# Scan, attention and a three-way gated layer on one core: the last part's product turned round, its result copied in halves, and a new order of the first two parts

## The chip, the core and the metric

One Trainium2 chip, one of its cores. Five engines work side by side, each with its own queue of instructions taken in order: TensorE (PE, with its weight loads, PEld), VectorE (DVE), ScalarE (ACT), GpSimd (POOL) and SyncE (SP), which here issues most transfers. They wait for one another by semaphores. The metric is the device time of one execution in microseconds (us).

## The reference

```python
def _attn_ref(r, k, v, w, u):              # r, k, v, w: (4, 8, 768, 48), u: (8, 48)
    state = zeros((B, H, D, D))
    for t in range(S):
        kt, vt, rt, wt = (k[:, :, t], v[:, :, t], r[:, :, t], w[:, :, t])
        cur = einsum('bhd,bhe->bhde', u[None] * kt, vt)
        y[:, :, t] = einsum('bhd,bhde->bhe', rt, state + cur)
        state = wt[:, :, :, None] * state + einsum('bhd,bhe->bhde', kt, vt)

def _moe_ref(x, w1, w2, w3, w_out):        # x: (3072, 384), w1..w3: (384, 768), w_out: (768, 384)
    h = maximum(maximum(x @ w1, x @ w2), x @ w3)
    return h @ w_out
```

The result of the recurrence, laid out as 3072 tokens by 384, is the input of the layer.

## The kernel before

**Tiling.** The recurrence is cut into 24 chunks (k = 0 to 23): six stretches of 128 time steps for each of four batches. The layer is cut into six parts ("halves" in the code) of 512 tokens; part h needs the four chunks of its stretch of time. For each part there are 18 products up (three weight matrices by six tiles f of 128 hidden columns), of which the maximum of three is tile f of h, and then the products down. Most layer products are done as three products of a high and a low half each (hi x hi, hi x lo, lo x hi); in part 0 the tiles f below 4 are done as one full product.

**The order.** The first two parts and the chunks up to 13 are issued by a written list, PARTS (line 79), read left to right; every engine takes its share of each step into its own queue in that order. After it a loop (line 802) issues parts 2 to 5 and the other chunks. The letters of the list, with the chunk's number behind them:

- Chunks: `n` loads (SP, L267). `b`, `f` scans (DVE, L406, L421), with `p` (POOL, L415) and `q` (DVE, L418) between. `r` scales r and k (DVE, L430). `c3` squares for a later check (ACT, L435). `d` multiplies k by u, for k below 8 in four ACT instructions (L443). `e` for k below 8 is 32 small products (PE, L460) and a copy (DVE, L463), then the loads of the next chunk's v (SP). `X` scores (PE, L489), `M` their copy (DVE, L496, and for some chunks ACT, L500, other columns of the same tile `grams`). `T` transposes (PE, L511; ACT copies to kn, L513). `R`, `V`, `Y` write the chunk's y (PE, L527, L593, L614); behind `V` ACT reads four elements (the touch, L598, L620), for which `Y` waits. `U` products for the state (PE, L551, L542), `m`, `S`, `Z` the state itself (L558, L563 or L566, L570). `E` copies y into x (ACT, L632, L636).
- Weights: `w` issues a load (SP, L329). `l` converts a pair of loaded weights (two ACT instructions, L346 and L347). `h` is DVE's part of it (L352), ahead of which it issues the conversions of a pair if `l` has not. `c` alone joins them (DVE, L358). `s` and `o` split a pair in high and low (ACT, DVE, L140, L141).
- Layer: `g` with a piece and a number is a group of products up of part 0 (`d`: the columns of chunks 0 and 1, `c`: of chunks 2 and 3, `e`: all), `G` of part 1, `D` and `H` are groups down of parts 0 and 1 (L211). `t` takes one finished group out of PSUM (ACT copy L158 the first time, DVE maximum L160 after). `x` splits x. `W10` is ten filler products on PE (L660).

Ahead of the list stand LEAD fillers of one column and WARM full ones (line 789). `grams` is a PSUM tile of two banks.

**The end.** In the last part the product down has h as the standing operand and w_out as the moving one (384 columns), so that rows are tokens: four tiles tt of 128 tokens. Tiles 0 and 1 are copied by ACT and stored by SP (L216, L765); tiles 2 and 3 (`late`) stay in PSUM. Behind the last group come BACK one-column fillers. Then every engine reads a flag (L820) and jumps over a second, slow way of computing everything (L821), which is there for inputs that the fast way cannot do. Behind the jump ACT copies tile 2 and DVE copies tile 3 (L932), and SP stores both (L933).

Of the kernel before, what the change touches and what calls it, by code (L numbers as in the profile page):

```python
# [44 lines left out]
C = 128  # L45
# [22 lines left out]
WARM = 9  # L68
LEAD = 69
BACK = 8  # L70
# [8 lines left out]
PARTS = """b0 w w p0 q0 f0 d0 b1 e0 p1 q1 R0 w d1 r0 W10 X0 c0 w T0 f1 W3 M0 b2 n3 p2 e1 r1 V0 q2 U0 W3 d2 l w X1 f2 w Y0 E0 M1  # L79
         T1 n4 h e2 R1 V1 r2 c1 c Y1 U1 w b3 E1 R2 X2 S1 l p3 T2 w M2 gd0 q3 d3 U2 V2 n5 h f3 c e3 c2 Y2 S0 t gd1 r3  # L80
         gd3 l T3 t X3 b4 p4 gd2 d4 E2 n6 U3 h q4 S2 M3 t c f4 R3 S3 e4 r4 V3 h gd4 gd5 c3 c T4 Y3 E3 Z4 X4 d5 t c4 U4
         M4 m4 b5 gd6 t w t gd7 p5 w q5 R4 n7 V4 S4 t b6 e5 f5 t gc1 t r5 gc7 Z5 p6 gc0 d6 t Z6 gc4 w t l T5 Y4 h X5
         c5 c w U5 q6 gc3 M5 f6 l gc2 b7 ge9 m5 E4 t p7 S5 gc5 h t c R5 q7 t h c e6 d7 r6 t x h V5 ge11 s gc8 t T6 l
         X6 o Y5 c h U6 ge10 ge13 t s o w t ge14 h w M6 m6 c E5 t s c o f7 S6 t t c6 Z7 n8 ge15 R6 V6 e7 h t gd8 w b8
         c ge16 ge12 r7 p8 ge17 w t t h c7 T7 X7 c l Y6 U7 E6 t d8 gc6 t t q8 s o l n9 D3 f8 D0 m7 s b9 Z8 r8 D4 p9 S7
         T8 R7 M7 q9 w f9 o V7 X8 Z9 Y7 U8 E7 n10 m8 e8 D1 l c8 D5 s x b10 d9 p10 l S8 o M8 D2 G12 r9 s t G13 G2 G0 t
         G14 G1 e9 o s t c9 T9 R8 V8 n11 w t X9 b11 q10 Y8 E8 f10 l U9 G4 t G3 o d10 w p11 m9 q11 t r10 e10 S9 M9 w
         f11 Z10 G6 c10 s l t G16 t r11 w T10 R9 o V9 n12 b12 t w p12 t w X10 s U10 M10 t Y9 o G15 q12 t G5 f12 t s
         Z11 o r12 G17 E9 d11 m10 S10 t t t s t G10 G7 T11 T12 e11 R10 V10 t d12 X11 Z12 U11 Y10 n13 G8 G9 c12 o c11
         m11 S11 M11 G11 t E10 R11 e12 t V11 X12 t U12 b13 t Y11 t E11 p13 H2 H5 H3 m12 x q13 H0 H1 w d13 H4 f13 M12  # L90
         n14 r13 e13 Z13 S12 c13"""
# [8 lines left out]
LATE = 2  # L100
# [12 lines left out]
def kernel(ctx: ExitStack, tc, tin, nat, u_flat, u_pair, v_t, w_flat, out, ytr):  # L113
# [16 lines left out]
    across = out[0:NH - 1].rearrange("h (k p t) -> h k p t", k=KT, p=128)  # L130
    natural = out[NH - 1].rearrange("(b p n) -> b p n", b=B, n=DM)
# [12 lines left out]
    def moe(x, pools, store, late=None, plain=0, turned=True):  # L144
# [7 lines left out]
        def take_up(f, ps, cols):  # L152
# [3 lines left out]
            n = taken[f, cols.start] = taken.get((f, cols.start), 0) + 1  # L156
# [42 lines left out]
        def downs():  # L199
            order = [(tt, f) for tt in range(KT if turned else CPH) for f in range(FT)]  # L200
            order.insert(FT, order.pop(FT - 1))
            wide_to = HT if turned else DM
            pss = {}
            for n, (tt, f) in enumerate(order):
# [4 lines left out]
                for i, (ht, wt) in enumerate(terms):  # L209
                    h, w = ht[f], wt[FT * 3 + f]  # L210
                    nc.tensor.matmul(pss[tt][:, 0:wide_to], lhsT=w[:, cut] if turned else h[:, cut],  # L211
                                     rhs=h[:, :] if turned else w[:, :],
                                     start=(f == 0 and i == 0), stop=(f == FT - 1 and i == len(terms) - 1))
                if f == FT - 1 and not (late and tt >= LATE):
                    o = mp.tile([128, HT], F32, name="m")[:, 0:wide_to]
                    nc.scalar.copy(out=o, in_=pss[tt][:, 0:wide_to])  # L216
                    store(tt, o)
# [603 lines left out]
    with tc.If(rv != 0), ExitStack() as slow:  # L821
# [99 lines left out]
        with tc.For_i(0, NH - 1) as half:  # L921
            again_moe(half, across, True)
# [80 lines left out]
```

## Time and profile before

| | us |
|---|---|
| median of three runs | 391.71 |
| the three runs | 391.2, 391.71, 394.22 |
| the profiled execution | 391.18 |
| its span, first to last instruction | 389.5 |
| PE busy in it | 381.7 (98%) |
| DVE busy | 265.9 (68%) |
| ACT busy | 173.4 (45%) |
| POOL busy | 85.2 (22%) |

An instruction's row names the line, the engine, the operation, and out<-in by the program's names. Idle time in square brackets or behind the bar is that of the engine ahead of the instruction, with what ended it. A "q" behind an engine's name is its sequencer.

### The profile page before, as it was taken

How to read it: one execution, taken by the hardware profiler on the slowest of the kernel's cores; microseconds unless marked ns; L12 is line 12 of the kernel's file. 1: busy time of each engine (PE TensorE's matmuls, PEld its weight loads, DVE VectorE, ACT ScalarE, POOL GpSimd, SP SyncE). 2: the span in 40 equal slices, each digit the busy share in tenths (PEclk: the TensorE clock that was granted, in tenths of full speed). 3: DMA queues.
4: the chain of work that ended last, by engine and by line, in shares of the span. 5: the costliest groups of instructions: out<-in, count | busy, mean ns of one | idle time of the engine just before them, and what ended most of it. 6: DMA issues, size and time to landing. Idle time of an engine off the chain costs nothing.

```text
span 389.5 us, 10503 instructions
## 1 busy us (share of the span) xinstructions
PE 381.7 (98%) x4480; PEld 309.3 (79%) x4480; DVE 265.9 (68%) x399; ACT 173.4 (45%) x373; POOL 85.2 (22%) x102
## 2 busy tenths in 40 slices
PE   8899999999999999999999999999999999999995
PEld 4688867766788888888888888888888887878895
DVE  7999999986779975598778567777568431432320
ACT  4688787643544443333444443443443332421210
POOL 3000000221443252144424314333414100000000
PEclk9999999999999999999999999999999999999999
DMA  7993897301823431477243866143951123200002
GB/s 284 403 347 103 284 406 248 112 2 52 272 68 126 147 127 51 136 292 223 68 173 115 275 198 210 61 168 98 307 201 44 42 82 89 94 3 1 0 24 67
DMA packets 23576, 58.44 MB, mean 150 GB/s; under 512 B 2720, under 2 KB 3712, under 8 KB 23520
## 3 DMA queue, kind: packets, MB, share of 16 engines
q1 hardware_dynamic: 20144, 48.58, 36.0%
q10 hardware_dynamic: 3376, 9.09, 7.3%
q8 instruction: 37, 0.61, 0.6%
q14 instruction: 19, 0.16, 0.1%
HBM read 51.87 MB, written 4.72 MB: 145 GB/s over the span
## 4 chain that ended last, share of the span: by engine, by line
PE 86%; DVE 6%; DMA 3%; ACT 2%; issue 2%; SPq 0%; POOL 0%; ACTq 0%; DVEq 0%
PE psm L175 53%; PE psm L211 18%; PE grams L489 3%; PE y L527 3%; PE y L614 3%; DMA w<-in_w_all_dram 2%; PE psm L511 2%; PE grams L542 1%; DVE w L358 1%; PE grams L460 1%; DVE cv L352 1%; PE grams L211 1%; PE y L211 1%; DMA tin<-in_tin_dram 1%; DVE w L141 1%
## 5 line engine op out<-in xcount | busy, mean ns | idle before, releaser
L175 PE MATMUL psm<-x_hi,w 128*128 128x512 f32 x576 | 183.0, 393 | 0.0
L175 PEld LDWEIGHTS psm<-x_hi,w 128*128 128x128 f32 x576 | 108.1, 188 | 23.5 <-issue 0.2
L175 PE MATMUL psm<-x_lo,w 128*128 128x512 f32 x288 | 112.1, 389 | 0.0
L160 DVE TENSOR_TENSOR m<-psm,m 128x512 f32<-128x512 f32 x64 | 43.7, 685 | 51.2 <-PE psm L175 44.2
L175 PEld LDWEIGHTS psm<-x_lo,w 128*128 128x128 f32 x288 | 54.1, 188 | 11.1 <-issue 0.2
L211 PE MATMUL psm<-h_hi,w 128*128 128x512 f32 x180 | 59.5, 430 | 0.3 <-DVE h_hi L160 0.3
L140 ACT CAST h_hi<-m 128x512 fp32r<-128x512 f32 x32 | 19.6, 617 | 54.6 <-DVE m L160 54.6
L211 PEld LDWEIGHTS psm<-h_hi,w 128*128 128x128 f32 x180 | 33.4, 188 | 12.1 <-issue 4.8
L470 POOL TENSOR_SCALAR_AFFINE_SELECT a<-sums 64x512 f32<-64x512 f32 x32 | 25.2, 787 | 72.3 <-DVE sums L467 71.3
L435 ACT ACTIVATE gf<-gf 112x1034 f32<-112x1034 f32 x24 | 25.7, 1070 | 26.4 <-DVE tin L430 26.2
L415 POOL TENSOR_SCALAR d_fwd<-gf 112x4 f32<-112x4 f32 x24 | 6.6, 276 | 134.6 <-DVE gf L406 128.3
L421 DVE TENSOR_TENSOR_SCAN gf<-tin,d_fwd 112x517 f32<-112x517 f32 x24 | 35.6, 1482 | 0.4
L406 DVE TENSOR_TENSOR_SCAN gf<-tin,d_bwd 112x517 f32<-112x517 f32 x24 | 30.2, 1258 | 5.7 <-DMA tin<-in_tin_dram 5.6
L175 PE MATMUL psm<-x,w 128*128 128x256 f32 (+1 forms) x126 | 33.9, 418 | 0.0
L430 DVE TENSOR_TENSOR tin<-tin,gf 112x1024 f32<-112x1024 f32 x24 | 31.1, 1296 | 0.0
L211 PE MATMUL psm<-h_lo,w 128*128 128x512 f32 x78 | 30.4, 390 | 0.0
L141 DVE TENSOR_TENSOR h_lo<-m,h_hi 128x512 fp32r<-128x512 f32 x32 | 23.9, 752 | 7.7 <-ACT h_hi L140 7.5
L175 PEld LDWEIGHTS psm<-x,w 128*128 128x128 f32 x126 | 23.0, 190 | 6.8 <-issue 3.3
L447 POOL TENSOR_TENSOR kr<-kr,u_bc 128x384 f32<-128x384 f32 x16 | 27.7, 1730 | 1.3
L141 DVE TENSOR_TENSOR x_lo<-x,x_hi 128x512 fp32r<-128x512 f32 x18 | 11.4, 685 | 22.7 <-ACT x_hi L140 22.7
L446 POOL TENSOR_TENSOR kr<-kr 128x384 f32<-128x384 f32 x16 | 22.9, 1434 | 9.4 <-DMA kr<-in_nat_dram 8.4
L382 ACT ACTIVATE cv<-cv,mid_top 128x384 f32<-128x384 uint32 x24 | 14.9, 621 | 16.6 <-DVE cv L380 16.5
(99 smaller groups left out, 468.6 us busy)
## 6 DMA issues: line engine op xcount, KB each, us to landing
tin<-in_tin_dram SPq DMA_DIRECT2D x24, 512.0 KB, 4.5
w<-in_w_all_dram SPq DMA_DIRECT2D x25, 384.0 KB, 7.6
w<-in_w_all_dram ACTq DMA_DIRECT2D x23, 384.0 KB, 3.4
v<-in_nat_dram SPq DMA_DIRECT2D x24, 288.0 KB, 5.4
tin<-in_tin_dram SPq DMA_DIRECT2D x24, 262.5 KB, 5.3
kr<-in_nat_dram SPq DMA_DIRECT2D x16, 384.0 KB, 5.1
out_dram<-m SPq DMA_DIRECT2D x15, 256.0 KB, 2.5
x<-x SPq DMA_DIRECT2D x10, 96.0 KB, 2.9
```

The costliest lines, as they stand in the source:

```text
L140: nc.scalar.copy(out=hi, in_=src)
L141: rest = lambda: nc.vector.tensor_tensor(out=lo, in0=src, in1=hi.bitcast(F32), op=ALU.subtract)
L160: nc.vector.tensor_tensor(out=m[:, cols], in0=ps[:, cols], in1=m[:, cols], op=ALU.max)
L175: nc.tensor.matmul(ps[:, cols], lhsT=wt[i][:, ct * 128:(ct + 1) * 128], rhs=x[part][:, ct, cols], start=(n == 0), stop=(n == KT * len(term ...
L211: nc.tensor.matmul(pss[tt][:, 0:wide_to], lhsT=w[:, cut] if turned else h[:, cut], rhs=h[:, :] if turned else w[:, :], start=(f == 0 and i ...
L406: nc.vector.tensor_tensor_scan(out=g[0:112, ::-1], data0=t[0:112, 0:WC][:, ::-1], data1=d_bwd[0:112, ::-1], initial=0.0, op0=ALU.mult, op1 ...
L421: nc.vector.tensor_tensor_scan(out=prep[k]["f"][0:112, :], data0=tbuf[k % NB][0:112, 0:WC], data1=d_fwd[0:112, :], initial=0.0, op0=ALU.mu ...
L430: nc.vector.tensor_tensor(out=both[0:112], in0=both[0:112], in1=by[0:112], op=ALU.mult)
L435: nc.scalar.activation(out=flat, in_=flat, func=AF.Square, accum_out=acc[0:112, k:k + 1])
L446: nc.gpsimd.tensor_tensor(out=n[:, 0, :], in0=n[:, 0, :], in1=n[:, 1, :], op=ALU.mult)
L447: nc.gpsimd.tensor_tensor(out=n[:, 0, :], in0=n[:, 0, :], in1=u_bc[:, :], op=ALU.mult)
L470: nc.gpsimd.affine_select(out=a[o:o + HC, 0:H, :], in_=cs[o:o + HC, :].unsqueeze(2).broadcast_to([HC, H, HC]), pattern=[[0, H], [1, HC]], ...
```

## The change

In the last part the product down has w_out as the standing operand and h as the moving one, like in the other parts: three tiles of 128 output columns by 512 tokens. Tiles 0 and 1 go out ahead of the jump, and the last one stays in `grams`, and is copied behind the jump in two halves of 256 columns, one by DVE and one by ACT, then stored by one transfer. The host puts the result in order. BACK goes from 8 to 5, WARM from 9 to 8, LEAD from 69 to 86. PARTS is a new order of the same steps, with fillers of 9, 4 and 5 products for 10, 3 and 3. The slow way loses its second body, and `take_up` gets an assertion that issues nothing.

```diff
-WARM = 9
-LEAD = 69
-BACK = 8
+WARM = 8
+LEAD = 86
+BACK = 5
...
-PARTS = """b0 w w p0 q0 f0 d0 b1 e0 p1 q1 R0 w d1 r0 W10 X0 c0 w T0 f1 W3 M0 b2 n3 p2 e1 r1 V0 q2 U0 W3 d2 l w X1 f2 w Y0 E0 M1
-         T1 n4 h e2 R1 V1 r2 c1 c Y1 U1 w b3 E1 R2 X2 S1 l p3 T2 w M2 gd0 q3 d3 U2 V2 n5 h f3 c e3 c2 Y2 S0 t gd1 r3
...
-         X6 o Y5 c h U6 ge10 ge13 t s o w t ge14 h w M6 m6 c E5 t s c o f7 S6 t t c6 Z7 n8 ge15 R6 V6 e7 h t gd8 w b8
-         c ge16 ge12 r7 p8 ge17 w t t h c7 T7 X7 c l Y6 U7 E6 t d8 gc6 t t q8 s o l n9 D3 f8 D0 m7 s b9 Z8 r8 D4 p9 S7
...
+PARTS = """w b0 d0 p0 q0 f0 b1 w R0 e0 p1 q1 W9 r0 w X0 d1 f1 c0 M0 W4 b2 T0 n3 e1 p2 l w W5 q2 r1 d2 f2 V0 X1 c1 M1 T1 h
+           Y0 U0 E0 b3 e2 w R1 r2 V1 U1 Y1 w c X2 h n4 S1 E1 w d3 T2 gd1 S0 w p3 M2 w U2 q3 l n5 R2 c V2 S2 w c2 t f3 e3
...
+           s t q7 X6 f7 o t d7 s l Y5 U6 c6 M6 gc4 t h c o m6 n8 h S6 l ge10 E5 b8 t ge12 h t ge13 t ge14 R6 s o t c p8 c
+           V6 e7 gc3 ge15 ge16 t l r7 t ge17 q8 t t h c T7 Y6 X7 s n9 f8 r8 E6 U7 o t c7 s D2 D3 D1 m7 b9 p9 o s q9 T8 R7
...
-LATE = 2
+LATE = KT - 1
...
-            order = [(tt, f) for tt in range(KT if turned else CPH) for f in range(FT)]
+            order = [(tt, f) for tt in range(KT) for f in range(FT)]
...
-                    h, w = ht[f], wt[FT * 3 + f]
-                    nc.tensor.matmul(pss[tt][:, 0:wide_to], lhsT=w[:, cut] if turned else h[:, cut],
-                                     rhs=h[:, :] if turned else w[:, :],
+                    nc.tensor.matmul(pss[tt][:, :], lhsT=wt[FT * 3 + f][:, cut], rhs=ht[f][:, :],
                                      start=(f == 0 and i == 0), stop=(f == FT - 1 and i == len(terms) - 1))
...
-    last = w_p.tile([128, 2, 2 * PC], F32, name=f"w{spot}")
-    for tt in range(LATE, CPH):
-        o = last[:, tt - LATE, 0:PC]
-        (nc.scalar.copy if tt < CPH - 1 else nc.vector.tensor_copy)(out=o, in_=left[tt][:, 0:DM])
-        nc.sync.dma_start(out=natural[tt], in_=o)
+    last = w_p.tile([128, 2, 2 * PC], F32, name=f"w{spot}")[:, 0, 0:HT]
+    nc.vector.tensor_copy(out=last[:, 0:HT // 2], in_=left[:, 0:HT // 2])
+    nc.scalar.copy(out=last[:, HT // 2:], in_=left[:, HT // 2:])
+    nc.sync.dma_start(out=across[NH - 1, LATE], in_=last)
```

`left` is `grams[:, 0, :]`, 512 columns of one bank.

## Rows read from the trace of the kernel before

**Rows 1.** The page: busy time, granted clock in 40 slices, chain by engine.
```profile
PE 381.7 (98%) x4480; PEld 309.3 (79%) x4480; DVE 265.9 (68%) x399; ACT 173.4 (45%) x373; POOL 85.2 (22%) x102
PEclk9999999999999999999999999999999999999999
PE 86%; DVE 6%; DMA 3%; ACT 2%; issue 2%; SPq 0%; POOL 0%; ACTq 0%; DVEq 0%
```
**Rows 2.** Timeline of PE, 71 to 86 us: start, us, instruction, idle before it.
```profile
72.23 0.69 PE L460 MATMUL grams<-tin,kr 48*64 48x64 f32 x32 [0.55 <-DVE scur L563]
...
85.66 0.70 PE L211 MATMUL psm<-h_hi,w 128*128 128x512 f32 x1 [0.26 <-DVE h_hi L160]
```
**Rows 3.** Timeline of ACT, 13 to 21 us.
```profile
13.35 1.28 ACT L443 ACTIVATE kr<-tin 112x128 f32<-112x128 f32 x4
14.54 1.02 ACT L346 ACTIVATE cv<-w,low_end 128x768 uint32<-128x768 uint16 x1
...
16.32 0.48 ACT L632 COPY x<-y 128x384 f32<-128x384 f32 x1
...
18.86 1.07 ACT L435 ACTIVATE gf<-gf 112x1034 f32<-112x1034 f32 x1
...
20.07 0.48 ACT L632 COPY x<-y 128x384 f32<-128x384 f32 x1
```
**Rows 4.** Timeline of PE, 0 to 24 us.
```profile
1.06 1.86 PE L658 MATMUL psm<-warm 128*1 128x1 bf16 x69 [1.06 <-POOL warm L274]
2.86 3.50 PE L660 MATMUL psm<-warm 128*128 128x512 bf16 x9
...
6.92 2.33 PE L660 MATMUL psm<-warm 128*128 128x512 bf16 x10
...
17.13 0.69 PE L460 MATMUL grams<-tin,kr 48*64 48x64 f32 x32 [0.31 <-ACT a L500]
...
21.82 1.47 PE L175 MATMUL psm<-x,w 128*128 128x256 f32 x6
```
**Rows 5.** The first two weight loads: issues, and time from issue to landing.
```profile
L329 SPq DMA_DIRECT2D w<-in_w_all_dram x2: 677/730/784, 4.6 to 5.5; - x2
...
DMA to landing us min/median/max: 8.3/8.4/8.5
```
**Rows 6.** Chain that ended last, 330 us on: start, us, what.
```profile
335.50 12.24 PE psm L175 x54
...
372.58 6.26 PE psm L211 x36
```
**Rows 7.** PE's jump, of the instructions of line 821: duration in ns, start.
```profile
L821 PEldq COMPARE_BRANCH x1: 4034/4034/4034, 383.8 to 383.8; - x1
```
**Rows 8.** Timeline of the end: SP, ACT and DVE.
```profile
379.44 0.33 SPq L765 DMA_DIRECT2D out_dram<-m  x1
...
382.49 0.48 ACT L932 COPY w<-y 128x384 f32<-128x384 f32 x1 [3.07 <-ACTq L821]
...
384.07 1.98 SPq L933 DMA_DIRECT2D out_dram<-w  x2
...
385.13 0.56 DVE L932 COPY w<-grams 128x384 f32<-128x384 f32 x1 [10.44 <-PE grams L211]
385.71 0.34 SPq L933 DMA_DIRECT2D out_dram<-w  x1
```
**Rows 9.** Timeline at 302 us: two engines read one PSUM tile (`M`).
```profile
301.78 0.73 DVE L496 COPY_PREDICATED a<-mask,grams 128x512 f32<-128x512 int32 x1
302.54 0.37 ACT L500 COPY a<-grams 128x256 f32<-128x256 f32 x1 [0.22 <-DVE a L496]
```
**Rows 10.** Groups by shape, ACT: count, busy us, mean ns, idle before.
```profile
L216 ACT COPY m<-psm 128x512 f32<-128x512 f32 x15 | 8.8, 585 | 19.7 <-PE psm L211 19.7
```
**Rows 11.** Stores ahead of the jump: count, size, median us to landing.
```profile
out_dram<-m SPq DMA_DIRECT2D x15, 256.0 KB, 2.5
...
out_dram<-m SPq DMA_DIRECT2D x2, 192.0 KB, 2.5
```

More of the change, by code (lines that the diff above doesn't have):

```diff
@@ L142, in split, with moe @@
         rest() if later is None else later.append(rest)
-    def moe(x, pools, store, late=None, plain=0, turned=True):
+    def moe(x, pools, store, late=None, plain=0):
         ps_m, hp, mp = pools
@@ L155, in take_up @@
             m = top[f]
-            n = taken[f, cols.start] = taken.get((f, cols.start), 0) + 1
+            n = taken.get((f, cols.start), 0) + 1
+            for at in range(cols.start, cols.stop, C):
+                assert taken.get((f, at), 0) == n - 1
+                taken[f, at] = n
             if n == 1:
@@ L225 @@
     ps_y = ctx.enter_context(tc.tile_pool(name="ps_y", bufs=1, space=PSUM))
-    left, spot = {}, NW // 2
+    spot, left = NW // 2, grams[:, 0, :]
     def late(tt):
-        both = grams if tt == CPH - 1 else ps_y.tile([128, 2, HT], F32, name="y")
-        left[tt] = both[:, 0, :]
-        return left[tt]
+        return left
     with ExitStack() as fast:
@@ L764, in store @@
             def store(tt, o):
-                nc.sync.dma_start(out=natural[tt] if half == NH - 1 else across[half, tt], in_=o)
-            up, catch_up, ups, down = moe(xs[half], pools, store, late if half == NH - 1 else None, plain=FR if half == 0 else 0,
-                                          turned=half < NH - 1)
+                nc.sync.dma_start(out=across[half, tt], in_=o)
+            up, catch_up, ups, down = moe(xs[half], pools, store, late if half == NH - 1 else None, plain=FR if half == 0 else 0)
             now = dict(half=half, up=up, catch_up=catch_up, ups=ups(), down=down())
@@ L801 @@
         groups = 2 * GPH
-        while groups < GPH * NH - DPH + 2 * CPH:
-            half = min(groups // GPH, NH - 1)
-            g = groups - half * GPH
+        while groups < GPH * NH:
+            half, g = divmod(groups, GPH)
             if g == 0:
@@ L903 @@
         yt = ytr.rearrange("k p b (h t) -> k p b h t", t=C)
-        def again_moe(half, of, turned):
+        with tc.For_i(0, NH) as half:
             x = xs_p.tile([128, KT, HT], F32, name="x")
@@ L914, in store2 @@
             def store2(tt, o):
-                nc.sync.dma_start(out=of[tt] if not turned else of[ds(half, 1), tt].rearrange("h p t -> (h p) t"), in_=o)
-            _, _, ups, down = moe(dict(hi=x_hi, lo=x_lo), pools, store2, turned=turned)
+                nc.sync.dma_start(out=across[ds(half, 1), tt].rearrange("h p t -> (h p) t"), in_=o)
+            _, _, ups, down = moe(dict(hi=x_hi, lo=x_lo), pools, store2)
             for part in (ups, down):
@@ L920, in again_moe @@
                     pass
[L921 to L933 removed]
+        back = pool("back", 1).tile([128, HT], F32, name="back")
+        nc.sync.dma_start(out=back[:, :], in_=across[NH - 1, LATE])
+        nc.vector.tensor_copy(out=left, in_=back[:, :])
+    last = w_p.tile([128, 2, 2 * PC], F32, name=f"w{spot}")[:, 0, 0:HT]
+    nc.vector.tensor_copy(out=last[:, 0:HT // 2], in_=left[:, 0:HT // 2])
+    nc.scalar.copy(out=last[:, HT // 2:], in_=left[:, HT // 2:])
+    nc.sync.dma_start(out=across[NH - 1, LATE], in_=last)
 def _layout(r, k, v, w, u, moe_w1, moe_w2, moe_w3, moe_w_out):
@@ L1000 @@
     y = res.results[0]["out_0_dram"]
[L1001 to L1002 removed]
+    return np.ascontiguousarray(y.reshape(NH, DM, B, C).transpose(2, 0, 3, 1)).reshape(B * S, DM)
```

34 lines of the change are left out of this document (12 added, 22 removed).

## The prediction

> **What bounds the kernel now.** I read the page first: busy shares, then the chain that ended last. TensorE (PE) is busy 98% of the 389.5 us span and carries 86% of the chain [rows 1]. So an edit gains only where PE waits or does filler, and a loss appears at once as a new hole on PE. Next I looked for those holes in the timeline of PE. After 25 us the first two parts show only two holes over a tenth of a microsecond: 0.55 us at 71.7 and 0.26 us at 85.4 [rows 2]. Real slack is left only in the first 22 us, where warmers fill PE, and at the end: the last copy begins at 385.13 and the span ends at 389.5. In the first 22 us I read ScalarE (ACT) and then PE, to see which engine paces the first chunks; for the end I read what each queue does from its last ordinary work to its first instruction behind the jump.
>
> **The first chunks in the new order.** In the old order ACT does, from 13.35 us: four products by u (d2), the two conversions of the first weight pair (`l`, L346 and L347), the copy of E0, the copy of M1. They stand shoulder to shoulder, and e2 on PE waits for the copy of M1 until 17.13 [rows 3, 4]. Nothing waited for weights: the second weight load was issued at 5.5 and took up to 8.5 us, so it was there at 14.0 [rows 5], when d2 still ran.
>
> The new order puts `l` ahead of d2 and ahead of the touch of V0, and c1 ahead of M1. The two loads stay where they were in SyncE's (SP's) queue (`w ... w ... e0`), so they land at 14.0 again. ACT's queue is strict, so ACT stands still until 14.0 with d2, touch, c1 and M1 behind it. Then, with the durations of the old order: the pair takes 1.78 (14.54 to 16.32), to 15.8; d2 1.19 (13.35 to 14.54), to 17.0; the touch a tenth, to 17.1; c1 1.21 (18.86 to 20.07), to 18.3 [rows 3]; the copy of M1 0.37 [rows 9], to 18.65. So e2 starts near 18.7 instead of 17.13.
>
> From e2 to the first expert product the old order took 4.7 us, to 21.82 [rows 4]. In the new order that product, gd1, reads x of chunks 0 and 1 and so waits for E1. ACT reaches E1 late: after M1 come T1's copy and E0 (about half a microsecond each, to 19.6), the touch of V1, which needs V1 on PE (in the old order 1.7 from e2's start to the end of that touch, 17.13 to 18.86; so 20.4), then a second pair, which `h` now issues here (1.78, to 22.2), S1 (0.3) and E1 (0.48): 23.0 to 23.1. The products done by then are the same set in both orders (e0 to e2, X0 to X2, T0 to T2, V, U, Y of 0 and 1), so gd1 at 23.1 against gd0 at 21.82 is a loss of **1.3**. Ends: 0, if ACT's delay lies wholly under other work, and 1.8, if e2's delay of 1.5 and one more copy (0.3) pass through. I take 1.3, which follows the queue. PE has almost no later holes in which to win it back [rows 2].
>
> The warmers themselves: LEAD adds 17 tiny products at 1.86/69 = 0.027, some 0.46; WARM takes one of 0.39 (3.50/9) away; the two are even. Fillers go from 16 to 18 products, two more of 0.22 (the ten at 6.92 took 2.33), ahead of V0 and X1, where PE would wait for r1 anyway [rows 4]. I take 0 for all of it; bare of that cover it is 0.43.
>
> **The two later holes.** The hole at 71.7 is e7 waiting for S6 on VectorE (DVE) [rows 2]. In the old order one expert group (ge15) lies between S6 and e7; in the new one ge10, ge12, ge13 and ge14, some 27 more products of 0.227 (12.24/54) [rows 6], about 6 us, and PE also comes 1.3 later. It closes. The hole at 85.4 is the first down product waiting for the last maximum of an h tile; in the old order gc6, which feeds it, stands just ahead of D3, in the new order gc3 has three whole groups behind it. It closes too: **minus 0.8**. Ends: nothing (another step waits there instead) and minus 0.8; and the order could open holes of its own, for which the largest here (0.55) and the sum of both are the nearest measure, so plus 0.8 as the other end.
>
> **The last part turned round.** Products go from 72 of 384 columns to 54 of 512. Old price 6.26/36 = 0.174, two further pieces of 18 alike, so 12.5; new price from the 512-column products just before, 12.24/54 = 0.227, so 12.24 [rows 6]. The last product ends 0.28 sooner, at about 384.85, and the copy that began at 385.13 [rows 8] could begin there. The loads of weights change sides and keep their 128 columns. The slow path, shortened, has no row in the trace, and the new assertion issues nothing.
>
> **The last copy.** DVE's 384 columns took 0.56 [rows 8]. Half of 512 is 256: between two thirds of that (0.37) and all of it; I take 0.41. ACT's 256 columns took 0.37 [rows 9]. Side by side the copies would end at 385.3. But both halves read one tile, `grams`. The trace has that case: DVE's L496 and ACT's L500 read different columns of `grams`, and ACT began 0.03 after DVE ended (302.54 after 301.78 + 0.73) [rows 9]. One after the other the halves end at 384.85 + 0.41 + 0.03 + 0.37 = 385.66, later than one whole copy of 0.56 would.
>
> The Trainium skill (PSUM — Partial Sum Buffer, section "PSUM bank collisions raise a hardware error") says that two engines must not touch the same bank and the same partitions at one time, reads by ScalarE and VectorE included, and that software has to keep them apart. By that rule the split gains nothing, the end of the copies being 385.66 and not 385.3, a difference of 0.36 wherever the store waits for them; the row on L500 agrees.
>
> **SP's jump.** The store must also wait for SP. SP issued its last ordinary store at 379.44, then read the flag, jumped, and issued its next store at 384.07: 4.63 later, though the copy for it was done at 382.97 (382.49 + 0.48) [rows 8]. In the new order the last ordinary store is tt=1's, after 36 of 54 products rather than 36 of 72: 36 x (0.227 - 0.174) = 1.9 later, and ACT copies 512 columns in 0.585 [rows 10] rather than 384 in 0.48, 0.1 more. So it leaves near 381.45, and SP can issue the final store only at 386.1. The old final store left at 385.71 [rows 8]. The gains of the PE and of the copy, in either form, are hidden behind this: **plus 0.4**. Ends: minus 0.4 (SP free, halves side by side, 385.3) and plus 0.5. ACT's own jump (3.07 idle ahead of its late copy [rows 8]) moves by the same 2.0 to about 384.5, still ahead of PE's end. One store of 256 KB for two of 192 KB: both sizes took 2.5 to land [rows 11], so 0.
>
> **Five tiny products.** PE's branch was recorded from 383.8 for 4.03, to 387.8 [rows 7], while the rest waited for the stores until 389.5. Three tiny products fewer (0.027 apiece [rows 4], so about 0.1) lie under that: 0. Uncovered, PE's jump would need to end over a microsecond later to count.
>
> **Sum.** Against the profiled execution (span 389.5, 391.18 in all): 1.3 - 0.8 + 0.4 = +0.9, so **392.1 us**. The three runs shown have a median of 391.71 and reach from 391.2 to 394.22, so this stands 0.4 above the median, inside their spread.
>
> **Rivals.** First: ACT's hole at the start costs nothing, both later holes close, and SP is the only loss: 391.18 - 0.8 + 0.4 = 390.8; with SP free 390.0. For it: PE did filler in that stretch. Against it: e2 and gd wait for ACT by name. Second, on the slower side: TensorE's lower clock. The granted clock is full in all 40 slices of the page [rows 1], yet the first nine full warmers took 0.39 apiece, near the pace of 1.2 GHz, and the ten at 6.92 took 0.23, that of 2.4, though PE had been issuing tiny products from 1.06 on [rows 4]. The new order leaves PE idle for about 1.5 us ahead of Y0 (T1 ends near 15.7, the touch comes at 17.1), where the old order's fillers left no hole over 0.31. If the clock falls there and its return costs what those nine cost more, 9 x 0.16 = 1.4, the time is 393.5. It decides once a hole is long enough for the clock to fall. Against it: no gap in the old trace let it fall, but none was that long.
>
> The Trainium skill (TensorE: Matmul & The Clock Gate, section "HAM oscillation — how this bites in real kernels") says that waits between bursts of matmuls can send the array back to half clock, each time paid anew; no run here shows whether 1.5 us is enough.
>
> Third: the new order opens holes of 1 to 2 us in the stretch from 30 to 100 us, where DVE is nearly full: 393 to 394. Fourth: the split and SP both come out well, start as forecast: 391.18 + 1.3 - 0.8 - 0.4 = 391.3.
>
> **Chances.** Forecast (391.5 to 392.7) 0.42; first rival 0.24; clock 0.10; new holes 0.14; fourth 0.10. Range 389.9 to 394.1: it takes in the first and fourth rivals and most of the holes, and leaves out about 0.15. One per cent is 3.9 us, about what a measurement of this kernel can tell from no change. All of PE's idle time over the span is 389.5 - 381.7 = 7.8 us [rows 1], over half of it behind the last product, so faster by more than 1% is very unlikely: 0.03. Slower by more than 1% needs the clock and the holes together: 0.06. Same: 0.91.
>
> **What would show it.** Right: L346's first run preceded by 1.5 us of ACT idle that a weight load ended; e2's L460 near 18.7 and the first L175 near 23.1; no holes at e7 or the first D; 54 last products at 0.227; ACT's half starting 0.03 behind DVE's; SP's final store near 386.1, after both halves. Wrong: a first L175 before 22; a hole over 0.5 us between 30 and 160; warmers of 0.39 after 15 us; a final store that leaves as soon as the copies end.

## The result

The changed kernel takes **393.78 us** (median of 22 executions, 392.29 to 398.52); the kernel before, in 22 executions beside it, 391.39 us (389.78 to 394.22). The ratio is 1.0069, interval 1.0054 to 1.0085: some 2.4 us more. That is within 1%, and within the range given (389.9 to 394.1); but it lies outside the forecast's own 391.5 to 392.7: the forecast stood 0.4 us above the median of the three executions known then, and the change came out 2.4 us above the median of 22. The profiled execution took 393.42 us with a span of 391.5, against 391.18 and 389.5. One execution, that of 398.52 us, counts as slow and is left out of the ratio.

The page of the changed kernel: busy time, granted clock in 40 slices, chain by engine.

```profile
PE 382.2 (98%) x4477; PEld 307.5 (79%) x4477; DVE 266.9 (68%) x399; ACT 172.5 (44%) x373; POOL 85.7 (22%) x102
...
PEclk9999999999999999999999999999999999999998
...
PE 93%; DVE 2%; DMA 1%; ACT 1%; POOL 1%; issue 1%; DVEq 0%; ACTq 0%; POOLq 0%
```

PE's busy time differs from [rows 1] by 0.5 us while the span is 2.0 longer: PE waits longer, and the page doesn't say where. So I cut both traces at the same four products and compare the pieces (us):

| piece | before | after | difference |
|---|---|---|---|
| start of the span to the first expert product | 21.82 | 22.44 | +0.62 |
| to the first down product (e7's hole lies in it, the hole of the first D at its end) | 61.70 | 60.79 | -0.91 |
| to the first product of the last down part | 288.90 | 290.38 | +1.48 |
| to the end of the span | 17.04 | 17.86 | +0.82 |

The last column adds up to the +2.0 of the span. Line numbers of the changed file differ by up to 12 from those of the file before (L346 is now L342, L175 is L176, L211 is L210, L821 is L815, L933 is L922).

**The start.** Timelines of ACT and PE, 13 to 23 us: start, us, what, idle before it.

```profile
13.74 1.02 ACT L342 ACTIVATE cv<-w,low_end 128x768 uint32<-128x768 uint16 x1 [1.31 <-DMA w<-in_w_all_dram]
...
16.64 0.14 ACT L594 COPY touch<-y 112x2 f32<-112x2 f32 x1
...
17.74 0.35 ACT L496 COPY a<-grams 128x256 f32<-128x256 f32 x1
```

```profile
16.83 0.45 PE L589 MATMUL y<-a,v 64*64 64x128 f32 x8 [0.82 <-ACT touch L594]
...
18.36 0.69 PE L456 MATMUL grams<-tin,kr 48*64 48x64 f32 x32
...
22.44 0.91 PE L176 MATMUL psm<-x,w 128*128 128x256 f32 x3
```

ACT waits 1.31 us for the weight load with d2, the touch, c1 and M1 behind it; PE waits 0.82 us for the touch, and e2 starts at 18.36 in place of 17.13 [rows 4]. From e2 to the first expert product half of that is won back.

**The middle.** Both holes of [rows 2] are gone: e7 and the first down product have no idle time in front of them (timeline of PE):

```profile
73.41 0.67 PE L456 MATMUL grams<-tin,kr 48*64 48x64 f32 x32
...
83.23 0.70 PE L210 MATMUL psm<-h_hi,w 128*128 128x512 f32 x1
```

One new hole stands far behind them, ahead of T11 (timeline of PE at 123 us):

```profile
123.24 0.60 PE L507 MATMUL psm<-ident,tin 112*128 112x112 f32 x4 [1.53 <-DVE tin L426]
```

T11 transposes what r11 (L426) has multiplied. The timelines of DVE and SP show why r11 is late:

```profile
115.98 0.55 DVE L463 TENSOR_REDUCE sums<-kr 128x8 f32<-128x384 f32 x1 [4.19 <-POOL kr L443]
...
119.99 1.93 DVE L417 TENSOR_TENSOR_SCAN gf<-tin,d_fwd 112x517 f32<-112x517 f32 x1
121.96 1.22 DVE L426 TENSOR_TENSOR tin<-tin,gf 112x1024 f32<-112x1024 f32 x1
```

```profile
103.39 4.60 SPq L267 DMA_DIRECT2D tin<-in_tin_dram  x2
108.08 1.80 SPq L254 DMA_DIRECT2D kr<-in_nat_dram  x1
```

SP's queue issues n11's load of `tin` at 103.39, but the second half of it must wait until PE has read the buffer, to 107.66. Behind it stands the load of `kr` for chunk 10, which e9 asks for. It leaves at 108.08 and lands at 113.70; POOL multiplies; DVE's sum (e10) waits 4.19 us for that, with f11 and r11 in the strict queue behind it. In the order before, e9 stands ahead of n11, and T11 started at 136.73 us in place of 123.24; no hole stands ahead of it there.

**The end.** Chain that ended last (start, us, what), and timelines of SP, DVE and ACT:

```profile
373.77 8.16 PE psm L210 x36
381.93 4.09 PE grams L210 x18
```

```profile
382.64 0.33 SPq L761 DMA_DIRECT2D out_dram<-m  x1
...
386.05 0.42 DVE L920 COPY w<-grams 128x256 f32<-128x256 f32 x1 [10.17 <-PE grams L210]
...
386.50 0.37 ACT L921 COPY w<-grams 128x256 f32<-128x256 f32 x1 [3.90 <-DVE w L920]
...
387.33 0.35 SPq L922 DMA_DIRECT2D out_dram<-w  x1
```

The 54 products take 8.16 + 4.09 = 12.25 us, where the 72 took 12.52. ACT's half starts 0.03 us after DVE's has ended and both are done at 386.88; SP issues the last store at 387.33, 4.70 us after its ordinary one. The DMA issues of the last 5 us, with the median time to landing:

```profile
out_dram<-w SPq DMA_DIRECT2D x1, 256.0 KB, 2.8
```

So by this one execution: start +0.6, two old holes -0.9, one new hole +1.5, SP's jump +0.4, the rest of the end +0.4. Single traces differ without any change: four with the old order reach their first expert product between 21.82 and 23.11 us. So these terms were put to the test.

### The profile page after: what moved, and what is told of

Same layout as the page of the kernel before. It is cut to its first block, busy times and chain, and to the rows that moved or that the text cites. A ratio compares the mean times of both kernels' runs of the same rounds, so it can differ in the third digit from the quotient of the medians.

```text
span 391.5 us, 10492 instructions
## 1 busy us (share of the span) xinstructions
PE 382.2 (98%) x4477; PEld 307.5 (79%) x4477; DVE 266.9 (68%) x399; ACT 172.5 (44%) x373; POOL 85.7 (22%) x102
## 4 chain that ended last, share of the span: by engine, by line
PE 93%; DVE 2%; DMA 1%; ACT 1%; POOL 1%; issue 1%; DVEq 0%; ACTq 0%; POOLq 0%
PE psm L176 57%; PE psm L210 19%; PE grams L485 3%; PE y L523 3%; PE y L610 3%; PE psm L507 2%; PE psm L656 2%; DMA kr<-in_nat_dram 1%; PE grams L538 1%; PE grams L456 1%; PE grams L210 1%; PE y L589 1%; PE psm L547 1%; DVE tin L426 1%; PE psm L654 1%
## 5 line engine op out<-in xcount | busy, mean ns | idle before, releaser
L176 PE MATMUL psm<-x_hi,w 128*128 128x512 f32 x576 | 183.1, 393 | 0.0
L176 PEld LDWEIGHTS psm<-x_hi,w 128*128 128x128 f32 x576 | 108.1, 188 | 23.6 <-issue 0.2
L176 PE MATMUL psm<-x_lo,w 128*128 128x512 f32 x288 | 112.1, 389 | 0.0
L210 PE MATMUL psm<-h_hi,w 128*128 128x512 f32 x204 | 66.7, 425 | 0.0
L176 PEld LDWEIGHTS psm<-x_lo,w 128*128 128x128 f32 x288 | 54.1, 188 | 11.1 <-issue 0.2
L210 PEld LDWEIGHTS psm<-h_hi,w 128*128 128x128 f32 x204 | 37.9, 188 | 12.4 <-issue 5.3
L466 POOL TENSOR_SCALAR_AFFINE_SELECT a<-sums 64x512 f32<-64x512 f32 x32 | 26.6, 833 | 71.1 <-DVE sums L463 66.6
L417 DVE TENSOR_TENSOR_SCAN gf<-tin,d_fwd 112x517 f32<-112x517 f32 x24 | 37.9, 1578 | 0.3
L210 PE MATMUL psm<-h_lo,w 128*128 128x512 f32 x90 | 35.1, 390 | 0.0
L176 PE MATMUL psm<-x,w 128*128 128x256 f32 (+1 forms) x126 | 33.7, 418 | 0.0
L426 DVE TENSOR_TENSOR tin<-tin,gf 112x1024 f32<-112x1024 f32 x24 | 30.5, 1269 | 0.1
L139 DVE TENSOR_TENSOR h_lo<-m,h_hi 128x512 fp32r<-128x512 f32 x32 | 22.5, 709 | 8.4 <-ACT h_hi L138 8.2
L176 PEld LDWEIGHTS psm<-x,w 128*128 128x128 f32 x126 | 23.1, 190 | 6.5 <-issue 3.3
L509 ACT COPY kn<-psm 128x448 f32<-128x448 f32 x20 | 10.6, 531 | 32.2 <-PE psm L507 32.2
L442 POOL TENSOR_TENSOR kr<-kr 128x384 f32<-128x384 f32 x16 | 21.3, 1329 | 9.8 <-DMA kr<-in_nat_dram 4.9
```

Of the source, the lines that this page charges most:

```text
L139: rest = lambda: nc.vector.tensor_tensor(out=lo, in0=src, in1=hi.bitcast(F32), op=ALU.subtract)
L176: nc.tensor.matmul(ps[:, cols], lhsT=wt[i][:, ct * 128:(ct + 1) * 128], rhs=x[part][:, ct, cols], start=(n == 0), stop=(n == KT * len(term ...
L210: nc.tensor.matmul(pss[tt][:, :], lhsT=wt[FT * 3 + f][:, cut], rhs=ht[f][:, :], start=(f == 0 and i == 0), stop=(f == FT - 1 and i == len( ...
L417: nc.vector.tensor_tensor_scan(out=prep[k]["f"][0:112, :], data0=tbuf[k % NB][0:112, 0:WC], data1=d_fwd[0:112, :], initial=0.0, op0=ALU.mu ...
L426: nc.vector.tensor_tensor(out=both[0:112], in0=both[0:112], in1=by[0:112], op=ALU.mult)
L442: nc.gpsimd.tensor_tensor(out=n[:, 0, :], in0=n[:, 0, :], in1=n[:, 1, :], op=ALU.mult)
```

## The experiments

Each time is a median of 12 executions (7 of `e6_act`, 11 of `e11_twolate_one`), beside the kernel before in the same group (391.13, 391.23 and 391.20 us for the three groups); the interval is that of the ratio to it.

**The change in two: the end alone, the order alone.** In `e1_tail` the changed file gets the order and the two numbers of before; in `e2_order` the file before gets the new ones:

```diff
 # e1_tail, against the changed kernel       # e2_order, against the kernel before
-PARTS = """w b0 d0 p0 q0 f0 b1 ..."""       -PARTS = """b0 w w p0 q0 f0 d0 ..."""
+PARTS = """b0 w w p0 q0 f0 d0 ..."""        +PARTS = """w b0 d0 p0 q0 f0 b1 ..."""
-WARM = 8                                    -WARM = 9
-LEAD = 86                                   -LEAD = 69
+WARM = 9                                    +WARM = 8
+LEAD = 69                                   +LEAD = 86
```

> The new end alone (last down part turned, one last copy in two halves, five small products ahead of the jump), with the order, the warmers and the lead of before. Theory A (the loss lies mostly in the order): everything up to the last down part runs as before, and only the end is later: 0.4 us because SP's jump makes the last store late, 0.3 us because the 128x512 store lands 2.84 us after its issue and not 2.50; +0.8 us against before, some 392.2. Theory B (the loss lies in the end, and what the order loses early is swallowed later): +2.4 us, the whole difference.

> The new order of the first two parts alone, with its 8 warmers and 86 small products, and the end of before. Theory A: the start of the last down part is as late as in the changed kernel, 1.2 us later than before (0.6 from the start, 1.5 from the hole ahead of T11, less 0.8 or 0.9 for the two holes that are gone), so +1.2 us. Theory B: no change beyond 0.4 us.

Measured: `e1_tail` 392.82 us, ratio 1.0026 (1.0008 to 1.0044); `e2_order` 391.27 us, ratio 1.0004 (0.9975 to 1.0032). By the medians the end costs more than theory A gave it (+1.7 us, not +0.8) and the order less (+0.1, not +1.2). The intervals are wider than that: in microseconds +0.3 to +1.7 for the end and -1.0 to +1.3 for the order. So the end alone is slower, by less than theory B's 2.4, and theory A is neither shown nor ruled out. In the trace of `e1_tail` the last store leaves 13.65 us after the start of the last down part, as in the changed kernel (13.72), but lands 3.36 us later, not 2.84. And in the trace of `e2_order` the hole ahead of T11 is only 0.59 us.

**The hole ahead of T11.** `e3_swap` changes SP's queue and nothing else; `e4_t11` gives PE work while r11 runs:

```diff
 # e3_swap
-... t X9 U9 n11 e9 t d10 ...
+... t X9 U9 e9 n11 t d10 ...
 # e4_t11
-... n12 m10 l t t T11 d11 t G6 G1 e11 ...
+... n12 m10 l t t G6 T11 d11 t G1 e11 ...
```

> The changed kernel with two neighbours of the order swapped (e9 ahead of n11), which changes nothing but the order of four loads on SP's queue. Theory A (the hole ahead of T11 comes from SP's queue: the tin load of n11 waits for R8 until 107.66 us and holds the kr load behind it, so that DVE's sum over kr waits until 115.98 with f11 and r11 behind it): kr is issued at about 103.4 and has landed by 108, DVE's sum no longer waits for 4.2 us, r11 ends before PE gets to T11 at 121.7, the hole of 1.54 us goes, -1.5 us against the changed kernel. Rival C (DVE has too much work ahead of r11 wherever kr comes, since T11 stands 14 us earlier in PE's work): the hole keeps over 1 us, and the time stays within 0.5 us of the changed kernel.

> The changed kernel with the group G6 moved from behind d11 to ahead of T11. The kr load stays late. Theory A and rival C both say that PE has work while r11 runs: the group is nine products of 0.227 us, 2.0 us, and the hole of 1.54 us goes, -1.5 us against the changed kernel, if nothing else is late. If what is late is more than r11 (theory D: DVE's whole queue runs 4 us late), the hole comes back at a later step that waits for DVE, and the gain is below 0.5 us.

Measured: `e3_swap` 393.40 us, ratio 1.0052 (1.0027 to 1.0077); `e4_t11` 393.42 us, ratio 1.0045 (1.0021 to 1.0069). Timelines of SP, DVE and PE in `e3_swap` (everything is 3.3 us later here, for the reason in the next experiment):

```profile
106.68 0.38 SPq L254 DMA_DIRECT2D kr<-in_nat_dram  x1
...
107.61 3.70 SPq L267 DMA_DIRECT2D tin<-in_tin_dram  x2
```

```profile
116.50 0.55 DVE L463 TENSOR_REDUCE sums<-kr 128x8 f32<-128x384 f32 x1 [0.60 <-POOL kr L443]
```

```profile
125.24 0.60 PE L507 MATMUL psm<-ident,tin 112*128 112x112 f32 x4 [0.22 <-DVE tin L426]
```

The load of `kr` leaves ahead of `tin`'s, DVE's wait falls from 4.19 to 0.60 us, the hole from 1.53 to 0.22. The four traces with this swap have 0.22, 0.41, 0.23 and 0.47 us ahead of T11 (`e3_swap`, `e7_swap_oldend`, `e8_onecopy`, `e10_best`), the four with n11 ahead of e9 and T11 in its place 0.59 to 1.91. That SP's queue makes most of the hole is shown; rival C is out. In `e4_t11` the hole ahead of T11 is gone too, but 0.65 us come back at 126.3, where an up product waits for a maximum on DVE: half of theory D. From the first expert product to the last down part the traces with the swap and a full clock there take 349.41, 349.89 and 349.62 us (`e3_swap`, `e7_swap_oldend`, `e8_onecopy`), the old order 350.60, 350.23, 350.26 and 350.24, the changed kernel 351.17 and `e2_order`, with the same order, 350.10. So the mended order wins some 0.7 us on the old one, near the 0.8 at which the two old holes were priced, and the swap gains 1.5 us against the one trace and 0.5 against the other. (`e10_best`, below, has the swap too and takes 350.93.) By the time of the whole kernel only some 0.4 us arrive, and the intervals of `e3_swap` and of the changed kernel overlap.

**The clock.** The profiled execution of `e3_swap` took 395.68 us, 2.3 above its median. The granted clock of the same stretch in it and in the changed kernel (the figure behind POOL's busy time is PEclk):

```profile
15.00:18.00 3.00, 1.27 (x40) 0.98 (x33) 2.35 (x3) 3.00 (x8) 0.00 (x0) 0.96 0.90 350
18.00:21.00 3.00, 3.00 (x52) 2.58 (x56) 1.24 (x1) 2.13 (x5) 0.22 (x1) 0.50 0.07 28
21.00:24.00 3.00, 3.00 (x76) 2.79 (x72) 2.05 (x3) 1.03 (x3) 0.00 (x0) 0.50 0.73 223
```

```profile
15.00:18.00 3.00, 2.18 (x63) 1.71 (x55) 2.25 (x4) 3.00 (x10) 0.00 (x0) 1.00 0.94 361
18.00:21.00 3.00, 3.00 (x110) 2.78 (x107) 2.91 (x4) 2.02 (x6) 0.22 (x1) 1.00 0.54 173
```

In `e3_swap`, from 18 to 24 us PE ran at 0.50, the lower level of 1.2 GHz. What stood ahead of it (timelines of ACT and PE):

```profile
14.87 1.03 ACT L342 ACTIVATE cv<-w,low_end 128x768 uint32<-128x768 uint16 x1 [2.22 <-DMA w<-in_w_all_dram]
```

```profile
17.96 0.70 PE L589 MATMUL y<-a,v 64*64 64x128 f32 x8 [1.73 <-ACT touch L594]
```

The weight load landed 1.1 us later than in the changed kernel's trace, the hole ahead of Y0 grew from 0.82 to 1.73 us, and behind it the clock was down. The first expert product came at 26.20 in place of 22.44: 0.9 of that is the longer hole, 2.8 the clock. The swap lies 80 us behind and cannot be the cause. The Trainium skill (TensorE: Matmul & The Clock Gate, section "HAM oscillation — how this bites in real kernels") tells of waits between bursts of matmuls that send the array back to half clock; the trace agrees as far as behind a wait of 1.73 us the granted clock was 0.50, though the waits in the page's example are longer than that.

How often this happens can be counted, since every execution has a mean granted clock. One of 0.994 or less was had by 7 of 129 executions with the old order (before in the three groups, `e1_tail`, `e9_twolate`, `e11_twolate_one`) and by 24 of 100 with the new one (the changed kernel without its execution of 398.52 us, and seven variants, among them 2 of 12 of `e2_order`). They take some 2.5 us more than the others of their kernel (1.3 to 3.2 by kernel). So the new order pays in a quarter of its executions what the old pays in a twentieth: about half a microsecond in the mean.

**The start's order on ACT.**

```diff
-... p2 l w W5 q2 r1 d2 f2 V0 X1 c1 M1 T1 h Y0 U0 E0 ...
+... p2 w W5 q2 r1 d2 f2 V0 l X1 M1 c1 T1 h Y0 U0 E0 ...
```

> The changed kernel with two steps of the start moved: l (the low pair, which on ACT waits for a weight load to land) from ahead of d2 to behind V0, and c1 from ahead of M1 to behind it. PE, DVE and SP keep their order; only ACT's changes. Theory A (at the start PE waits for ACT, and ACT for the weight load that lands between 13.7 and 14.8 us): the hole of 0.8 us ahead of Y0 at 16.0 goes, e2 starts near 17.3 in place of 18.4, the first up product 0.6 us sooner or a little less; -0.6 us against the changed kernel, and executions in which a late landing makes PE wait longer and its clock fall after 16 us become rarer. Rival E (the weight chain is itself the limit: the join behind l comes later, and the first up product waits for it): the hole moves to the first up product, and the time stays within 0.3 us of the changed kernel or gets worse.

Measured: 393.65 us, ratio 1.0056 (1.0029 to 1.0083): no gain to be seen. Timeline of PE:

```profile
16.70 0.45 PE L589 MATMUL y<-a,v 64*64 64x128 f32 x8
...
19.43 0.44 PE L589 MATMUL y<-a,v 64*64 64x128 f32 x8 [0.50 <-issue]
...
22.88 1.35 PE L176 MATMUL psm<-x,w 128*128 128x256 f32 x5
```

The hole ahead of Y0 is gone, as theory A says, but 0.50 us stand ahead of Y's next run, and from T1 on PE to the first expert product it is 6.71 us, where the six traces with the start as it was and a full clock there (7.03 in the changed kernel) take 6.37 to 7.08: no gain. The hole moved, as rival E says, though not to the product that it named. Executions with a low clock are not rarer either (3 of 12): the hole ahead of T11, which is still in this kernel, brings the clock down as well. In this trace and in that of `e6_act` it was 1.91 and 1.87 us long, and behind it the clock fell; `e6_act` by stretches:

```profile
122.00:124.00 2.00, 0.41 (x4) 0.39 (x4) 1.97 (x3) 0.00 (x0) 0.00 (x0) 1.00 0.95 369
124.00:126.00 2.00, 2.00 (x8) 1.44 (x7) 0.58 (x2) 1.35 (x2) 0.00 (x0) 0.71 0.52 196
126.00:128.00 2.00, 2.00 (x6) 1.62 (x5) 1.97 (x4) 0.59 (x2) 0.00 (x0) 0.50 0.02 7
```

In the traces here holes up to 1.53 us passed without a fall; those of 1.73, 1.87 and 1.91 did not. In the two traces the first part's down to the second's took 67.6 us, 2.0 more than in the changed kernel, 0.4 of it the longer hole.

**The end: whose queue stores.**

```diff
-    nc.sync.dma_start(out=across[NH - 1, LATE], in_=last)
+    nc.scalar.dma_start(out=across[NH - 1, LATE], in_=last)
```

> The changed kernel with the last store issued from ACT's queue in place of SP's. Theory A (SP is late: its jump begins only after the ordinary store of the part before and ends 0.45 us after the last copy): ACT is through its jump by 385.7, so the store is issued within 0.1 us of the end of its own copy, 0.4 us sooner; -0.4 us against the changed kernel, from the start of the last down part 13.3 us to the store in place of 13.7. Rival F (the 0.45 us are the way from ACT's copy to any queue, not SP's jump): the store is as late as before, no change.

Measured: 394.32 us, ratio 1.0083 (1.0049 to 1.0118). The store left 13.59 us after the start of the last down part, not 13.3. Rival F's outcome, but by neither cause. Instructions of the jump's line (duration in ns, first and last start), and timeline of ACT:

```profile
L815 SPq EVENT_SEMAPHORE  x8: 17/17/17, 388.6 to 389.1; - x8
...
L815 ACTq EVENT_SEMAPHORE  x1: 17/17/17, 387.6 to 387.6; - x1
```

```profile
388.44 0.37 ACT L921 COPY w<-grams 128x256 f32<-128x256 f32 x1 [3.90 <-DVE w L920]
389.14 0.36 ACTq L922 DMA_DIRECT2D out_dram<-w  x1
```

ACT is through its jump at 387.6 and its copy ends at 388.82. But SP comes back from its own jump at 388.6 and raises eight semaphores, the last at 389.1, and the store on ACT's queue waits for three of them, among them those of two earlier stores: it follows within 0.05 us. SP is late, as the prediction said; another queue doesn't escape it. (In the changed kernel's trace the eight run from 386.6 to 387.1, and the store follows at 387.33.)

**The order mended, with the end of before; the end with one copy.** `e7_swap_oldend` is `e2_order` with the swap of `e3_swap`; `e8_onecopy` is the changed kernel with that swap, ACT's queue and this copy:

```diff
-    nc.vector.tensor_copy(out=last[:, 0:HT // 2], in_=left[:, 0:HT // 2])
-    nc.scalar.copy(out=last[:, HT // 2:], in_=left[:, HT // 2:])
+    nc.scalar.copy(out=last, in_=left)
```

> The new order, warmers and lead with the end of before, and e9 ahead of n11. Theory A: the order's hole ahead of T11 is gone and the end costs nothing, so from the first up product to the start of the last down part 1.2 us less than before (349.4 against 350.6), the start up to 0.6 us later, the end as before: -0.6 to -1.0 us against before, some 390.3. Theory B (the end is all): as before, within 0.4 us.

> The changed kernel with e9 ahead of n11, the last store issued from ACT's queue, and the last copy undivided on ACT (128x512 at 0.59 us). Theory A (the two engines take the one tile one after the other, 0.42 and 0.37 us with a gap of 0.03, so that the division costs time): the copy ends 0.2 us sooner than the halves, and the store is issued 13.05 to 13.1 us after the start of the last down part in place of 13.7; with the order mended -1.6 us against the changed kernel. Rival G (the division saves time, as two halves at once would): the copy ends later than the halves did, by 0.1 us or more.

Measured: `e7_swap_oldend` 391.34 us, ratio 1.0009 (0.9987 to 1.0032), no gain on before; `e8_onecopy` 393.40 us, ratio 1.0070 (1.0040 to 1.0099). The 0.7 us that the first wins in the middle go to the start (first expert product at 23.10) and to the clock (2 of 12). In the second the copy ended 13.02 us after the start of the last down part, 0.25 sooner than the halves (13.27), but the store left at 13.52, again right behind SP's last semaphore: the copy, in either form, is hidden. Its store landed 3.54 us after its issue. That made the landing the question.

**The end: two results behind the jump.** The new end, but with a second result left for behind the jump, as the kernel before leaves one, so that SP jumps after the first result's store and the last store has another ahead of it:

```diff
-LATE = KT - 1
+LATE = KT - 2
...
+    for tt in range(LATE, KT):
+        o = last[:, tt - LATE, 0:HT]
+        if tt < KT - 1:
+            nc.scalar.copy(out=o, in_=left[tt])
+        else:
+            nc.vector.tensor_copy(out=o[:, 0:HT // 2], in_=left[tt][:, 0:HT // 2])
+            nc.scalar.copy(out=o[:, HT // 2:], in_=left[tt][:, HT // 2:])
+        nc.sync.dma_start(out=across[NH - 1, tt], in_=o)
```

In `e11_twolate_one` the `else` goes and every `o` is copied whole on ACT. Both have the order of before.

> The new end alone (order, warmers and lead of before), but with two of the three last results left for behind the jump as the kernel before leaves two: the second is copied on ACT and stored there too, the third in halves as in the changed kernel. SP then jumps from behind the first result's store, 3.4 us sooner. Theory A (the new end's loss is SP's jump, 0.4 us, and a last store that goes alone and lands 2.8 to 4.0 us after its issue, where the last of before's pair needs 2.3 to 2.5): from the start of the last down part 13.3 us to the last store's issue in place of 13.7, its landing 2.3 to 2.5 us, -1.3 us against the new end alone, within 0.3 us of before. Rival H (the landing is long because the store has 2,048 bytes in a row in place of 1,536): the store is sooner, but still lands in 3 us or more; -0.4 us against the new end alone. Rival J (the products of 512 columns or the tile's place in memory cost what is lost): no change against the new end alone.

> The kernel of the run with two results behind the jump, with the last copy undivided on ACT in place of the halves. Theory A (halves go one after the other, 0.83 us together): the copy ends 13.02 us after the start of the last down part in place of 13.27, and as SP no longer hides it, the last store is issued 0.25 us sooner; -0.2 to -0.3 us against the halves, some 0.2 us below before. Rival: what hides a copy is now something else than SP's jump (ACT's own), and nothing changes.

Measured: `e9_twolate` 392.31 us, ratio 1.0036 (1.0014 to 1.0057); `e11_twolate_one` **390.99 us**, ratio 1.0003 (0.9983 to 1.0022). The stores behind the jump in `e9_twolate`, each with KB and time to landing:

```profile
out_dram<-w SPq DMA_DIRECT2D x1, 256.0 KB, 3.8
...
out_dram<-w SPq DMA_DIRECT2D x1, 256.0 KB, 2.1
```

A store of 256 KB lands in 3.81 us when it is the first behind the jump and in 2.09 when another went 3.1 us ahead of it. All traces of this study, from the start of the last down part (us):

| end | last store issued | its landing takes | span ends |
|---|---|---|---|
| before, and its end in two more traces | 13.29, 13.29, 13.29 | 2.50, 2.31, 2.37 | 17.04, 16.84, 16.90 |
| new end, halves, SP (5 traces) | 13.65 to 13.95 | 2.84 to 3.61 | 17.86 to 18.62 |
| new end, ACT's queue (2 traces) | 13.52, 13.59 | 3.54, 3.97 | 18.36, 18.87 |
| two results late, halves | 13.30 | 2.09 | 16.69 |
| two results late, one copy (2 traces) | 13.05, 13.05 | 2.02, 2.25 | 16.37, 16.60 |

Theory A is borne out by the traces, and rival H falls: the size is not what makes the landing long. A store that goes alone behind the jump lands 2.84 to 3.97 us after its issue; one that follows another lands in 2.02 to 2.50. What counts is to be the first behind the jump: the first stores of the six pairs take 3.35 to 3.81 us, of 192 KB and of 256 KB alike.

The DMA packets of these traces, taken one by one, show what the lone store waits for. DMA queues of the changed kernel from 385.5 us on (packets, MB, share):

```profile
q1 hardware_dynamic: 144, 0.26, 15.9%
q14 instruction: 2, 0.02, 1.5%
q8 instruction: 1, 0.02, 1.3%
```

In the seven traces with a lone store, 135 or 136 of its 144 packets have ended 1.70 us after its issue at the latest. In that time q8 carries one packet of 16 KB of instructions, which ends 1.40 to 2.52 us after the issue; the last packet of the store ends 0.99 us behind it, in every one of the seven. Nine packets are a sixteenth of the store, so by these times one of the 16 DMA engines carries the instructions ahead of its share of the store. For the later store of a pair that packet has ended 0.67 us after the issue at the latest, or begins only when the store's packets have nearly all ended. No run takes the packet away, so this is read from times and not tried.

With SP free the division costs the 0.25 us that the copies differ by. By the time, the mends of the end are not clear of the noise: `e9_twolate` is 0.5 us below the new end alone, not 1.3, and the intervals of the two overlap (the traced execution of `e9_twolate` was the second fastest of its 12, that of `e1_tail` the second slowest; 2 of the 12 of `e9_twolate` had the low clock). `e11_twolate_one` is 1.8 us below the new end alone by the medians, with intervals that still overlap; its own reaches to both sides of the kernel before. The Trainium skill (DMA: Bandwidth & Descriptors, section "Anatomy of one DMA — SWDGE (gpsimd) path") gives transfers issued by GpSimd a fixed cost of about 2.0 us that scales with nothing, which with its rate would make 2.6 for this size (an estimate). These are issued by SP, and the traces show no constant: stores of this size behind the jump take 2.0 to 4.0 us.

**All mends together.** `e10_best`: the new order with the swap, the end of `e11_twolate_one`, and PE's hole at 16 us filled:

```diff
-... T1 h Y0 U0 E0 b3 e2 ...
+... T1 h W4 Y0 U0 E0 b3 e2 ...
```

> The new order with e9 ahead of n11 and four warmers put ahead of Y0, where PE waited 0.8 to 1.7 us at 16 us, with 8 warmers and 86 small products at the start, and the end with two results behind the jump and one undivided last copy. Theory K (in the new order the hole at 16 us, whose length goes with the landing of a weight load, lets the clock fall in a part of the executions, 9 of 36 with the hole ahead of T11 mended, each some 2.5 us): with the hole filled, 0 or 1 of 12 executions have a mean granted clock below 0.993, and the others are as before or up to 1 us faster, 390.3 to 391.2. Rival L (the clock falls for another reason, or for the hole that comes behind the warmers): 3 of 12 executions or more have the low clock again.

Measured: 391.85 us, ratio 1.0017 (1.0005 to 1.0030). Not one of 12 executions had a mean clock below 0.996, as theory K says. It does not prove it: in this group the kernel before had no low clock either (0 of 29, against 5 of 65 in the two other groups), and no kernel with the hole left open ran beside it. Timeline of PE, where the hole was:

```profile
16.20 1.03 PE L657 MATMUL psm<-warm 128*128 128x512 bf16 x4
17.16 0.45 PE L590 MATMUL y<-a,v 64*64 64x128 f32 x8
```

The time is still 0.65 above before: in this trace 0.34 us of a new hole at 45.9 and smaller ones between 30 and 50 us, and 0.47 ahead of T11, undo what the order won. Theory K's second half (up to 1 us faster) did not come. Of all variants only `e11_twolate_one`, with the old order, has a median below that of the kernel before, and by its ratio the two are level.

## Why the prediction held, and where it was too low

That the time fell within the range was in part luck. The forecast's own bounds were passed, and the range took the time in because it had been drawn for the first, the third and the fourth rival; the third gave 393 to 394 for holes alone, while the measured time is made of smaller holes, a late landing and a clock that falls now and then. One of the prediction's own signs of being wrong, a hole over 0.5 us between 30 and 160 us, appeared at 121.7 us.

- **The start, +1.3.** The mechanism was right: ACT waits for the weight load (1.31 us, forecast 1.5), e2 comes at 18.36 (18.7). The size was off. The second leg, e2 to the first expert product, took 4.08 us and not 4.4, and the base was one execution: the old order's first expert product stands at 21.82 [rows 4], but at 23.11, 22.21 and 22.59 in the three other traces with that order, the new one's at 22.44, 22.68, 22.46, 22.53, 22.68 and 23.10. The means differ by 0.2 us (without `e3_swap`, whose 26.20 has the low clock in it). The first rival (the start costs nothing) was nearer.
- **The two later holes, -0.8.** Right: both closed, -0.91 in the profile.
- **Holes of the order's own.** The +0.8 kept as an end was the right thought in the wrong size, and the third rival had the kind and the price (1 to 2 us) with the wrong place: the hole came at 121.7 us, not between 30 and 100. What the prediction did not follow is SP's queue past e9 and n11, though a load that waits there holds all behind it. This term is +1.5 in the profile, and 0.6 to 1.9 in the four traces that keep n11 ahead of e9 and T11 in its place.
- **The last part, the copies, the jump.** Products 12.25 us (12.24), halves one after the other with 0.03 between (0.42 + 0.37, forecast 0.41 + 0.37), SP 4.70 us from store to store (4.63), the last store +0.43 late (+0.4): all as worked out, and the fourth rival (split and SP come out well) fell. The rule of the Trainium skill that the prediction named (PSUM — Partial Sum Buffer, section "PSUM bank collisions raise a hardware error") is agreed with by the 0.03 between the halves. But the 0.36 that hung on it never counted: the copies end before SP.
- **The landing, 0.** This step failed: a landing of 2.5 us, the same for one store as for two. I took it from the ordinary stores [rows 11] for the last one. The row to look at was that of the first store behind the jump, which the trace of before has at 384.07 [rows 8], and it landed 3.68 us after its issue:

```profile
out_dram<-w SPq DMA_DIRECT2D x1, 192.0 KB, 3.7
```

  In the kernel before the last copy and a second store come behind this one; the change makes a store of that kind the last thing that happens. It costs +0.34 in the profile and 0.76 in the mean of the five traces with halves (3.15 against 2.39).
- **The clock, a rival with 0.10.** In the profiled execution it did not fall, in a quarter of all executions it did, at a price of 1.6 to 2.8 us in the three traces that caught it (priced at 1.4). The decisive point, a hole long enough, was named rightly; that the hole differs between executions was not thought of. In the seven traces with this start it is 0 to 1.73 us long, by when the weight load lands (13.61 to 14.79) and how far PE has come by then.

Taken together, the forecast of +0.9 against the profiled execution had +1.3 too much by some 0.7 to 1.1 at the start, and left out 1.5 for the hole ahead of T11 and 0.3 to 0.8 for the landing. What stays open: the medians of `e2_order` and the changed kernel apart give less for the order (+0.1) than their traces do, and that the packet of instructions makes a lone store land later was read from traces, not tried. Two results left for behind the jump change two things at once, SP's earlier jump and a store ahead of the last one, and the runs do not part them.

## What to carry over

Before a step is moved, follow each queue that it is moved past, the loads included: a load that waits for a buffer holds all loads behind it, and the engine that pays can be two engines and 15 us away. Price the last store by the row of a store in the same place, the first behind the jump, and let SP jump early enough that another store goes ahead of it. And where an engine waits for a load, ask what a late landing does to PE: a hole that is harmless in one execution can be longer in the next and bring the clock down.

## Not expected of the hardware

A store of 256 KB took 2.02 to 2.25 us to land with another store some 3 us ahead of it behind the jump, and 2.84 to 3.97 alone, where its last packet ended 0.99 us behind a packet of 16 KB of instructions in all seven traces. A jump keeps SP 2.65 us from branch to the next instruction (383.95 to 386.60) and costs another 0.6 us in eight semaphores, three of which the last store waits for on ACT's queue too (389.14 in `e6_act`). And the granted clock was down, at 1.2 GHz, behind single waits of PE of 1.73, 1.87 and 1.91 us, in `e3_swap` from 18 to 24 us of full work.
